# Merging the mixer's work into three bursts per batch instead of four, and moving the low-rank adds to suit

## The chip, the cores and the metric

The kernel runs on one core of a Trainium2 chip. The metric is the device time of one execution in microseconds (us). Kernels are compared only within the same rounds.

Engine names in profile lines: PE is TensorE (matmuls), PEld its weight loads, DVE VectorE, ACT ScalarE, POOL GpSimd, SPq the queue of SyncE, from which all DMA transposes are issued.

## The reference

```python
# 8 batches, S = 3136 rows, D = 256, d_qk = 64, rank 32
scores = (1/S) * z @ z.T
x = u * (relu(scores)**2 @ v)                 # gated attention
h = x.T @ U @ V                               # low rank, along the sequence
w = x + h.T
out = w + relu(w @ w_ch1) @ w_ch2             # channel mixer, 256 -> 1024 -> 256
```

## The kernel before

A batch has 25 tiles of 128 rows (the last has 64). A "turn" computes the attention output of one tile: 24 pairs of matmuls, each 64 rows deep, the two halves of the array running side by side into two PSUM banks (in the trace the two of a pair mostly start 2 to 4 ns apart, and the next pair 109 ns after the first). Two tiles form a pair that shares a set of two banks (`sets[0]`, `sets[1]`, used alternately). (PSUM is the memory that the matmuls here write; its tiles are `ps` in the profile.) The set that no open pair uses is "spare"; low-rank adds and the mixer's down steps use it. The mixer takes a batch in seven chunks of two to four tiles. While the turns of batch b run, the mixer of batch b-1 is put between them, in bursts. After turn 0, the "rank block" (L479) makes `x.T @ U` of batch b-1. `_spread` distributes the score matmuls (`fill`) evenly among the steps of a turn (`main`).

For blocks on one side of the diagonal a turn reads "strips": transposed copies of scores already made, one DMA transpose per turn, issued four turns ahead (five buffers). The same queue also transposes the mixer's input (`turn_x`, tile `ut`, one per chunk) and z of the next batch (`turn_z`, tile `zT`, two pieces).

```python
def turn(b, o):                                  # strip for output tile o
    strip = strip_pool.tile([P, HALF, P], BF16, name="strip")
    transpose(out=strip, in_=A[o][:, P:])        # SP queue, DMA transpose

def close_pair(b, o):
    nc.scalar.copy(out=both[:, :w], in_=banks[1][:, :w])            # L385
    nc.vector.tensor_tensor(both, banks[0], both, add)              # L386
    ...
    nc.vector.tensor_tensor(x_at(b, t0, n), both, u_sb, mult)       # L395

def low_rank(b, c, ps=None, turned=True):        # arguments shortened
    ps = spare() if ps is None else ps
    ...                                          # 4 matmuls into both banks
    for h in range(2):
        nc.vector.tensor_tensor(q, ps[h], q, add)                   # L545
    if turned:
        turn_x(b, c)                             # DMA transpose x -> ut

def extend_z(b):
    zT = zT_of(b)
    nc.vector.tensor_copy(out=zT[:, NT:, :], in_=zT[:, :HALF, :])   # L238
...
burst_at = {4: (0, 1), 8: (2, 3), 13: (4, 5), 17: (6, 7)}
ahead = dict(zip((2, 3, 6, 7, 10, 11, 14), range(NC)))   # turn -> chunk
for i in range(begin, NT):
    o = turns(i)
    ...
        if b and i == 7:
            turn_z(b + 1, ((FIRST, NF),))
        if b and i == 10:
            turn_z(b + 1, ((0, FIRST),))
        if i == 11:
            extend_z(b + 1)
    main = attend_steps(b, o)
    if b and i in ahead:
        main.insert(17 if (i + (i > FIRST)) % 2 == 0 else 10,
                    lambda c=ahead[i]: low_rank(b - 1, c))
    _spread(main, fill)
    ...
        turn(b, turns(i + AHEAD))                # AHEAD = 4
    ...
    for n in burst_at.get(i, ()) if b else ():
        up, down = bursts[n]      # up of chunk n, down of chunk n-1
        steps = [down.pop(0)] if n == 4 else []
        steps += _merge(up, down)
        ...
        run(steps)
```

An up step is four matmuls (line L563) and a ReLU on ACT; a down step is eight matmuls (L608). L371 is attention, L298 scores, L531 low rank, L405 the quarter-size matmuls of the short tile (turn 12).

Of the kernel before, what the change touches and what calls it, by code (L numbers as in the profile page):

```python
# [18 lines left out]
def _spread(main, filler):  # L19

    n, m = len(main), len(filler)
    k = 0
    for i, step in enumerate(main):
        step()
        while k < m and (2 * k + 1) * n <= (i + 1) * 2 * m:
            filler[k]()
            k += 1
    for step in filler[k:]:
        step()


def _merge(*lists):

    keyed = [
        ((i + 0.5) / len(part), n, s)
        for n, part in enumerate(lists)
        for i, s in enumerate(part)
    ]
    return [s for _, _, s in sorted(keyed, key=lambda e: e[:2])]
# [3 lines left out]
def kernel(  # L43
# [28 lines left out]
    FIRST = HALF  # L72
# [27 lines left out]
    def spare():  # L100

        return sets[(opened[0] + (0 if acc else 1)) % 2]
# [29 lines left out]
    def turns(i):  # L132
        return (FIRST + i) % NT
# [4 lines left out]
    def col(t):  # L138
        return place(t) * P
# [10 lines left out]
    NC = len(chunks)  # L150
    offset = {t: (n, k) for n, c in enumerate(chunks) for k, t in enumerate(c)}

    def group(b, c):
        n = len(chunks[c])
        flat = x_bf[:, ((XB // 4) * b + c) % (XR // 4), : n * D]
        return flat.rearrange("p (a t c) -> p a t c", a=ND, c=P)
# [6 lines left out]
    def split(ap):  # L163
        return ap.rearrange("p (t a c) -> p t a c", a=ND, c=P)
# [4 lines left out]
    def load_z(b, parts):  # L169
        if b not in z_raw:  # L170
            z_raw[b] = stage.tile([P, NT, dqk], BF16, name="z_c")
        z_c = z_raw[b]
        for t0, t1 in parts:
            pool_dma(out=z_c[:, t0:t1, :], in_=rows(z[b])[:, t0:t1, :])
            if t1 == NF:
                for r in halves:
                    pool_dma(out=z_c[r, NF, :], in_=z[b, NF * P :, :])
# [14 lines left out]
    def turn_z(b, parts):  # L192
        z_bf = z_tiles[b]
        for t0, t1 in parts:
            transpose(
                out=zT_of(b)[:, t0 : upto(t1), :],
                in_=z_bf[:, t0 : upto(t1), :, :].rearrange("p t h c -> p (t h c)"),
            )
# [37 lines left out]
# [4 lines that stand above are left out]
    def load_v(b, part):  # L240
        t0, t1 = part
        v_bf = v_both[b % 2]
        if t0 < NF:
            pool_dma(out=v_bf[:, t0:t1, :], in_=rows(v[b])[:, t0:t1, :])  # L244
        else:
            for r in halves:
                pool_dma(out=v_bf[r, NF, :], in_=v[b, NF * P :, :])
# [67 lines left out]
    def score_steps(b, j, k0=0, k1=NB):  # L315
        steps = []
        n = (k1 - k0) * P
        parts = _ceil_div(n, 1024)
        each = n // parts
        h = each // 2  # L320
        for i in range(parts):
            at = k0 * P + i * each

            def step(at=at):
                dst = A[j][:, at : at + each].rearrange("p (i h) -> p i h", i=2)
                score(b, [(j, j * P + at + i * h, h, dst) for i in range(2)])

            steps.append(step)
        return steps

    def turn(b, o):
        strip = strip_pool.tile([P, HALF, P], BF16, name="strip")
        transpose(out=strip, in_=A[o][:, P:])
        strips[b, o] = strip
# [165 lines left out]
    def turn_x(b, c):  # L500
        n = len(chunks[c])
        ut = ut_pool.tile([P, ND * 512], BF16, name="ut")
        ut = ut[:, : ND * n * P].rearrange("p (a w) -> p a w", a=ND)
        transpose(
            out=ut.rearrange("p a (t c) -> p (a t) c", c=P),
            in_=group(b, c).rearrange("p a t c -> p a (t c)"),
        )
        uT[c] = ut
# [15 lines left out]
    def low_rank(b, c, ps=None, turned=True):  # L524

        ts = chunks[c]
        ps = spare() if ps is None else ps
        where = [(0, 0), (1, 0)] if len(ts) == 2 else [(0, 0), (0, 1), (1, 0), (1, 1)]
        order = sorted(zip(where, ts), key=lambda e: (e[0][1], e[0][0]))
        for (h, k), t in order:  # L530
            mm(  # L531
                out=ps[h][:, k * D : (k + 1) * D],
                lhsT=V_bf[halves[h], col(t) : col(t) + P],
                rhs=t1[b][halves[h], :],
                start=True,
                stop=True,
            )
        n = len(ts)
        x = group(b, c)
        dst = x.rearrange("p a t c -> p t a c")  # L540
        for h in range(2):
            ks = [k for (g, k), _ in zip(where, ts) if g == h]
            k0 = len(ks) * h if n == 2 else 2 * h
            q = dst[:, k0 : k0 + len(ks)]
            nc.vector.tensor_tensor(out=q, in0=split(ps[h][:, : len(ks) * D]), in1=q, op=ALU.add)  # L545
        if turned:
            turn_x(b, c)
# [92 lines left out]
    def bursts_of(b):  # L640

        out_ = []
        for c in range(NC + 1):
            alone = c == 0 or (c == NC - 1 and b == B - 2)
            up = [lambda s=s, c=c, a=alone: up_steps(c, a)[s]() for s in range(NH // 2)]
            up = up if c < NC else []
            down = down_steps(b, c - 1) if c else []
            out_.append((up, down))
        return out_
# [177 lines left out]
    def run(steps):  # L827
        for s in steps:
            s()
# [5 lines left out]
    for b in range(B):  # L835
        more = b + 1 < B
        begin = 0 if b else 2 * NG
        bursts = bursts_of(b - 1) if b else []
        burst_at = {4: (0, 1), 8: (2, 3), 13: (4, 5), 17: (6, 7)}
        own = own_at if b else first_at  # L840
        v_at = dict(zip((9, 11, 13, 15, 18, 21), V_PARTS[3:]))
        ahead = dict(zip((2, 3, 6, 7, 10, 11, 14), range(NC)))
        for i in range(begin, NT):
            o = turns(i)
            fill = [s for key in own.get(i, ()) for s in score_steps(b, *key)]
            if more:
                fill += [s for key in next_at[i] for s in score_steps(b + 1, *key)]
                if b and i == 1:
                    load_z(b + 1, WHOLE)
# [4 lines that stand above are left out]
                if b == 0 and i in v_at:  # L854
                    load_v(b + 1, v_at[i])
                if i == 11:
                    extend_z(b + 1)
            main = attend_steps(b, o)
            if b and i in ahead:
                main.insert(17 if (i + (i > FIRST)) % 2 == 0 else 10, lambda c=ahead[i]: low_rank(b - 1, c))  # L860
            _spread(main, fill)
            if b == 0 and i in first_turns:
                for t in first_turns[i]:
                    turn(b, t)
            elif i + AHEAD < NT:
                turn(b, turns(i + AHEAD))
            elif more:
                turn(b + 1, turns(i + AHEAD - NT))
            elif i == NT - AHEAD:
                turn_x(b, 0)  # L870
            if b == 0 and i in puts:
                puts[i]()
            if b and i == 0:
                rank_once(b - 1, spare()[0])
            for n in burst_at.get(i, ()) if b else ():
                up, down = bursts[n]
                if not more and n >= NC - 1:
                    late += up + (down if n == NC else [])
                    up, down = [], (down if n < NC else [])

                steps = [down.pop(0)] if n == 4 else []
                steps += _merge(up, down)
                if more:
                    loads = [lambda k=k: load_v(b + 1, V_PARTS[k]) for k in ((n,) if n < NC else (n, n + 1))]
                    steps = _merge(steps, loads)
                    if n == 1:
                        for k, part in ((6, (FIRST, NF)), (3, (0, FIRST))):
                            steps.insert(k, lambda part=part: double_z(b + 1, (part,)))
                run(steps)
# [4 lines left out]
    b = B - 1  # L894
# [45 lines left out]
```

## Time and profile before

| | before |
|---|---|
| median of 3 runs | 1004.49 us |
| PE busy | 984.2 us of 1003.0 (98%) |
| time from one batch's rank block (L479) to the next | 121.24 us, 5 of 6 within 0.25 |
| PE waiting for strips, whole run | 2.7 us |
| granted PE clock | 1.0 |

First, the busy times from the page of the kernel before.

```profile
PE 984.2 (98%) x13688; PEld 776.2 (77%) x13688; DVE 550.6 (55%) x1002; ACT 612.3 (61%) x835; POOL 171.8 (17%) x317
```

The costliest waits of PE in the kernel before: engine, tile and line of the waiting instruction, what it waited for, then us in total, how many times, and the longest.

```profile
PE ps L298 <- ACT A L311: 3.3, 5, 1.0
PE ps L371 <- DMA strip<-A: 2.7, 2, 2.1
PE ps L371 <- DVE A L313: 2.0, 4, 0.9
```

PE is the bottleneck and hardly waits.

Part of the trace that the change aims at: the second of two low-rank adds in successive turns (start in us, duration, engine, line, operation, and how many such instructions were merged into the row). The bracket is PE's idle time and what ended it.

```profile
260.54 0.27 PE L531 MATMUL ps<-t_sb,V_bf 64*128 64x256 bf16 x1
260.96 0.29 PE L531 MATMUL ps<-t_sb,V_bf 64*128 64x256 bf16 x2 [0.16 <-DVE x_bf L545]
```

From start to start PE loses 0.316 us more than usual here; the profile's bracket is smaller because it counts from the modelled end of the matmul before. Below, "gap" means start to start, less the usual distance.

### The profile page before, as it was taken

How to read it: one execution, taken by the hardware profiler on the slowest of the kernel's cores; microseconds unless marked ns; L12 is line 12 of the kernel's file. 1: busy time of each engine (PE TensorE's matmuls, PEld its weight loads, DVE VectorE, ACT ScalarE, POOL GpSimd, SP SyncE). 2: the span in 40 equal slices, each digit the busy share in tenths (PEclk: the TensorE clock that was granted, in tenths of full speed). 3: DMA queues.
4: the chain of work that ended last, by engine and by line, in shares of the span. 5: the costliest groups of instructions: out<-in, count | busy, mean ns of one | idle time of the engine just before them, and what ended most of it. 6: DMA issues, size and time to landing. Idle time of an engine off the chain costs nothing.

```text
span 1003.0 us, 31017 instructions
## 1 busy us (share of the span) xinstructions
PE 984.2 (98%) x13688; PEld 776.2 (77%) x13688; DVE 550.6 (55%) x1002; ACT 612.3 (61%) x835; POOL 171.8 (17%) x317
## 2 busy tenths in 40 slices
PE   7899999999999999999999999999999999999998
PEld 5678777787778877788787887778878788777855
DVE  6868754457544665456644566445663457542342
ACT  7877764667645776466755667466664667633154
POOL 5111112111121211221112211112111120011000
PEclk9999999999999999999999999999999999999999
DMA  9999989999798999999999997989989998678442
GB/s 177 186 196 206 175 153 186 169 198 173 149 205 165 170 160 181 178 179 168 156 185 174 188 162 149 192 177 179 170 156 181 181 183 152 127 152 166 99 98 97
DMA packets 414646, 167.94 MB, mean 167 GB/s; under 512 B 389472, under 2 KB 399136, under 8 KB 414512
## 3 DMA queue, kind: packets, MB, share of 16 engines
q1 hardware_dynamic: 385280, 99.68, 62.9%
q0 software_dynamic: 29232, 66.28, 28.5%
q8 instruction: 107, 1.75, 0.7%
q14 instruction: 27, 0.22, 0.1%
HBM read 61.88 MB, written 25.69 MB: 87 GB/s over the span
## 4 chain that ended last, share of the span: by engine, by line
PE 90%; DVE 4%; ACT 3%; DMA 2%; issue 0%; POOL 0%; DVEq 0%; ACTq 0%; POOLq 0%
PE ps L371 46%; PE ps L608 17%; PE ps L563 17%; PE ps L298 6%; ACT A L311 3%; DVE A L313 1%; PE ps L405 1%; DMA strip<-A 1%; DVE x_bf L545 1%; PE ps L531 1%; DMA z_c<-in_z_dram 1%; PE ps L479 1%; DMA zT<-z_bf 1%; DVE both L386 1%; DVE x_bf L395 0%
## 5 line engine op out<-in xcount | busy, mean ns | idle before, releaser
L311 ACT ACTIVATE A<-ps 128x832 bf16<-128x832 f32 (+9 forms) x477 | 359.1, 768 | 156.1 <-PE ps L298 149.6
L371 PE MATMUL ps<-v,A 64*128 64x256 bf16 x4988 | 341.8, 270 | 2.4 <-DVE A L313 1.1
L313 DVE TENSOR_TENSOR A<-A 128x832 bf16<-128x832 bf16 (+9 forms) x477 | 244.6, 527 | 131.2 <-ACT A L311 128.0
L371 PE MATMUL ps<-v,strip 64*128 64x256 bf16 x4420 | 307.4, 269 | 3.6 <-DMA strip<-A 2.7
L371 PEld LDWEIGHTS <-A 64*128 64x128 bf16 x4988 | 246.8, 94 | 45.8 <-issue 11.2
L581 ACT ACTIVATE relu_bf<-ps 128x1024 bf16<-128x1024 f32 (+2 forms) x206 | 186.0, 911 | 140.8 <-PE ps L563 138.7
L371 PEld LDWEIGHTS <-strip 64*128 64x128 bf16 x4420 | 222.8, 94 | 37.4 <-DMA strip<-A 4.6
L619 DVE TENSOR_TENSOR o_sb<-ps,x_bf 128x512 f32<-128x512 f32 (+1 forms) x104 | 69.7, 670 | 246.2 <-PE ps L608 223.8
L608 PE MATMUL ps<-w_bf,relu_bf 128*128 128x256 bf16 (+1 forms) x1600 | 201.5, 273 | 0.2 <-ACT relu_bf L579 0.2
L563 PE MATMUL ps<-ut,w_bf 128*128 128x512 bf16 (+2 forms) x896 | 198.3, 353 | 1.1 <-DVE x_bf L545 1.0
L608 PEld LDWEIGHTS <-relu_bf 128*128 128x128 bf16 (+1 forms) x1600 | 152.3, 98 | 46.6 <-issue 4.6
L563 PEld LDWEIGHTS <-w_bf 128*128 128x128 bf16 x896 | 85.0, 98 | 63.4 <-issue 7.7
L355 POOL DMA_DIRECT2D u_sb<-in_u_dram x96 | 53.7, 559 | 456.1 <-DVE x_bf L395 440.8
L298 PE MATMUL ps<-zT 64*128 64x416 bf16 (+8 forms) x812 | 131.7, 312 | 0.0
L385 ACT COPY both<-ps 128x512 f32<-128x512 f32 (+1 forms) x104 | 58.9, 566 | 73.8 <-PE ps L371 66.4
L632 POOL DMA_DIRECT2D out_dram<-o_sb x84 | 46.0, 548 | 278.2 <-DVE o_sb L619 274.9
L386 DVE TENSOR_TENSOR both<-ps,both 128x512 f32<-128x512 f32 (+1 forms) x104 | 69.4, 667 | 27.5 <-ACT both L385 26.7
L395 DVE TENSOR_TENSOR x_bf<-both,u_sb 128x512 bf16<-128x512 f32 (+1 forms) x104 | 69.8, 672 | 3.6
L545 DVE TENSOR_TENSOR x_bf<-ps,x_bf 128x512 bf16<-128x512 f32 (+1 forms) x112 | 65.4, 626 | 8.1 <-PE ps L531 8.0
L298 PEld LDWEIGHTS <-zT 64*128 64x128 bf16 x812 | 43.2, 94 | 3.9
L244 POOL DMA_DIRECT2D v<-in_v_dram x61 | 34.1, 561 | 1.2 <-DMA w_bf<-in_moe_w_ch_dram 1.1
L298 PE MATMUL ps<-relu_bf 64*128 64x416 bf16 (+9 forms) x121 | 22.2, 332 | 4.1 <-ACT A L311 3.3
(54 smaller groups left out, 207.9 us busy)
## 6 DMA issues: line engine op xcount, KB each, us to landing
u_sb<-in_u_dram POOLq DMA_DIRECT2D x96, 256.0 KB, 4.1
out_dram<-o_sb POOLq DMA_DIRECT2D x84, 256.0 KB, 3.2
v<-in_v_dram POOLq DMA_DIRECT2D x57, 192.0 KB, 5.1
strip<-A SPq DMA_TRANSPOSE x196, 5.6
out_dram<-o_sb SPq DMA_DIRECT2D x12, 256.0 KB, 2.0
z_c<-in_z_dram POOLq DMA_DIRECT2D x7, 384.0 KB, 5.7
u_sb<-in_u_dram POOLq DMA_DIRECT2D x16, 64.0 KB, 2.9
ut<-x_bf SPq DMA_TRANSPOSE x56, 3.6
```

The costliest lines, as they stand in the source:

```text
L298: mm(out=ps[:, k, :n], lhsT=zT[halves[k], j, :], rhs=zT_flat[halves[k], c : c + n], start=True, stop=True,)
L311: nc.scalar.activation(out=dst, in_=src, func=AF.Relu, scale=sc)
L313: nc.vector.tensor_tensor(out=dst, in0=dst, in1=dst, op=ALU.mult)
L371: mm(out=acc[t0][h][:, (o - t0) * D : (o - t0 + 1) * D], lhsT=w[halves[h]], rhs=v_both[b % 2][halves[h], j, :], start=start, stop=stop, **kw,)
L385: nc.scalar.copy(out=both[:, :w], in_=banks[1][:, :w])
L386: nc.vector.tensor_tensor(out=both[:, :w], in0=banks[0][:, :w], in1=both[:, :w], op=ALU.add)
L395: nc.vector.tensor_tensor(out=x_at(b, t0, n), in0=split(both[:, :w]), in1=u_sb[:, :n, :].rearrange("p t (a c) -> p t a c", c=P), op=ALU.mult,)
L545: nc.vector.tensor_tensor(out=q, in0=split(ps[h][:, : len(ks) * D]), in1=q, op=ALU.add)
L563: mm(out=ps[i][:, :w] if apart else ps[:, i, :w], lhsT=w1_bf[:, db, (hp + i) * P : (hp + i + 1) * P], rhs=uT[c][:, db, len(chunks[c]) * P ...
L581: nc.scalar.activation(out=relus[c][:, hp : hp + 2, :w], in_=ps[:, :, :w], func=AF.Relu)
L608: mm(out=ps[r, k * D : (k + 1) * D], lhsT=relus[c][:, ht, q : q + (TAIL if two else P)], rhs=w2_bf[:, ht, :], start=(ht < 1 + two), stop=( ...
L619: nc.vector.tensor_tensor(out=o_sb[:p, :nk, :].rearrange("p t (a c) -> p t a c", c=P), in0=split(ps[:p, : nk * D]), in1=x_at(b, t, nk)[:p] ...
```

## The change

The intent is fewer changes between attention and mixer on PE, and low-rank adds placed so that every chunk is ready for its earlier burst.

```diff
-        burst_at = {4: (0, 1), 8: (2, 3), 13: (4, 5), 17: (6, 7)}
+        burst_at = {4: (0, 1, 2), 11: (3, 4, 5), 16: (6, 7)}
...
-        ahead = dict(zip((2, 3, 6, 7, 10, 11, 14), range(NC)))
+        ahead = dict(zip((1, 2, 3, 6, 7, 10, 14), range(NC)))
...
-                main.insert(17 if (i + (i > FIRST)) % 2 == 0 else 10, lambda c=ahead[i]: low_rank(b - 1, c))
+                at = 17 if (i + (i > FIRST)) % 2 == 0 or i == 1 else 12
+                main.insert(at, lambda c=ahead[i]: low_rank(b - 1, c))
```

## The prediction

> **What bounds the kernel.** TensorE. The profile's first part has PE busy 984.2 of 1003.0 us (98%), ScalarE 612, VectorE 551; the chain of waits is 90% PE; PE's own waits sum to about 14 us. In the steady state one batch takes 121.3 us (PE's timeline). DMA is busy but PE almost never waits for it.
>
> **What recurs in each of the 7 mixed batches (gaps between matmul starts, PE's timeline).**
> - Attention uses 64-row matmuls, two at a time (about 109 ns a pair); the mixer uses 128 rows (109 ns for 256 columns). Crossing from one form to the other takes 200 to 205 ns instead of 109: about 93 ns lost, near one 94 to 98 ns weight load. [...] The batch has 8 such crossings for four bursts and 2 for the quarter-tile turn (i=12).
> - The second of two consecutive low-rank adds (i=7) stalls 316 ns: its PSUM set waits for VectorE (L545) of i=6.
>
> **The change.** Only order; no instruction is added or removed.
> 1. One burst fewer, and the second burst (after i=11) runs straight into the quarter turn. Crossings fall by three: 3 x 93 ns = 0.28 us a batch, **-2.0 us** in all.
> 2. Low-rank adds of second turns go from step 10 to 12 (some 0.22 us later), and i=6 now has the small chunk: the 316 ns stall should go, **-2.2 us**.
> 3. The first low-rank add is now at i=1, step 17, in the set that i=2 opens. PE reaches that opening about 1.15 us after the add begins (own 0.22, seven pairs, one score). VectorE[...] has a square (L313, 0.59 us) just ahead, then the two adds, 0.69 us each, overlapping slightly: it is done about 1.9 us after the add begins. PE is in order, so it stalls about 0.75 us: **+5.3 us**.
> 4. Bursts after i=11 and i=16 now begin at the end of a pair. Their first down-projection writes bank 1 of the set just closed, which ScalarE must first copy (0.58 us, from 0.1 us after the turn's end); only one up step (0.44 to 0.55 us) covers it: about 0.2 us each, **+2.8 us**.
> The queue of DMA transposes waits for PE far more than the reverse: no cost there.
>
> **Sum.** -4.2 + 8.1: +3.9 us on 1004.49: **1008.4 us**, 8 in 10 between 1002.5 and 1012.5. Chances: faster by over 2% 0.01, within 2% 0.97, slower by over 2% 0.02.
>
> **What would show it.** (1) 21 instead of 28 bursts, with crossings still near 200 ns. (2) No 316 ns gap at low-rank matmuls. (3) PE at L371 waiting for VectorE x_bf (L545), seven times 0.5 to 0.9 us, some 3 us after each rank block: a new line in PE's waits of about 5 us. (4) PE at L608 waiting for ScalarE both (L385), some 13 times about 0.2 us.
>
> **What would make it wrong.** VectorE free earlier at i=1 (the square done before the add) would shrink 3 to 0.2 us and make the change a gain of 1 to 3 us. Stalls on strips, or output stores bunching in a longer burst, would make it worse.

Two passages about the hardware that no trace of this case shows are cut from this text, and the cuts are marked. No term of the sum went with them: -4.2 + 8.1 still comes to +3.9 us. The order that point 3 counts on is seen in the trace of the kernel before: DVE ran two squares (L313, from 258.69 us) and only then the two adds (L545, from 259.63 us), and while the low-rank matmul of 260.96 us waited for DVE, PE started no other: its last start was at 260.54 us.

## More of the kernel before

Now the queue of DMA transposes in the kernel before, from turn 6 to turn 12 of one batch (start in us, duration in the queue, engine, line, operation, and how many such instructions were merged into the row).

```profile
260.94 1.23 SPq L504 DMA_TRANSPOSE ut<-x_bf  x1
262.26 2.47 SPq L333 DMA_TRANSPOSE strip<-A  x1
264.78 1.45 SPq L195 DMA_TRANSPOSE zT<-z_bf  x1
266.33 1.93 SPq L504 DMA_TRANSPOSE ut<-x_bf  x1
268.35 7.08 SPq L333 DMA_TRANSPOSE strip<-A  x3
281.57 1.76 SPq L195 DMA_TRANSPOSE zT<-z_bf  x1
285.33 1.67 SPq L504 DMA_TRANSPOSE ut<-x_bf  x1
```

From 260.9 to 275.4 us the queue is full: two ut, four strips and a zT one behind the other. PE ran the burst after turn 8 from 266.0 to 278.7 us. In those 12.7 us PE needs no strip, so the queue caught up and stood idle from 275.4 to 281.6.

## The result

The changed kernel took 1037.27 us (median of 6 runs, 1035.07 to 1041.62) against 1003.74 us, ratio 1.0335 with a 95% interval of 1.0303 to 1.0368: slower, far above the range. Its batches take 125.0 to 127.5 us (mean 126.4) instead of 121.2. Granted clock: 0.995.

Busy times from the page of the changed kernel:

```profile
PE 992.1 (96%) x13648; PEld 791.3 (76%) x13688; DVE 551.4 (53%) x1002; ACT 612.8 (59%) x835; POOL 171.5 (17%) x317
```

DVE and ACT do the same work. (40 matmul records are missing from this trace, all L563, so PE's real busy time is a little higher.) The waits of PE in the changed kernel:

```profile
PE ps L371 <- DMA strip<-A: 15.0, 10, 3.1
PE ps L608 <- ACT both L385: 4.1, 7, 0.7
PE ps L608 <- DVE both L386: 4.1, 3, 2.3
PE ps L298 <- ACT A L311: 3.2, 5, 1.0
PE ps L371 <- DVE x_bf L545: 2.3, 7, 0.3
```

The rows for L385 and L545 were predicted in kind; their sizes come below. The rows for strips (15.0 us, from 2.7) and for L386 were not. The queue of transposes in the changed kernel, from the last strips before the stretch on, shows why:

```profile
248.15 7.22 SPq L333 DMA_TRANSPOSE strip<-A  x3
274.57 1.21 SPq L504 DMA_TRANSPOSE ut<-x_bf  x1
275.87 1.35 SPq L333 DMA_TRANSPOSE strip<-A  x1
277.28 2.03 SPq L195 DMA_TRANSPOSE zT<-z_bf  x1
279.40 1.75 SPq L504 DMA_TRANSPOSE ut<-x_bf  x1
281.24 7.62 SPq L333 DMA_TRANSPOSE strip<-A  x3
288.95 3.15 SPq L195 DMA_TRANSPOSE zT<-z_bf  x1
292.20 1.26 SPq L504 DMA_TRANSPOSE ut<-x_bf  x1
```

From turn 6 on it is the same order as before, and the durations are alike (strips 7.62 us for three, before 7.08). But PE is no longer in a burst meanwhile: turns 5 to 11 run from 266.7 to 289.3 us without a break, and the next burst comes after turn 11. The queue is filled for 17.1 of the 17.6 us from 274.57 to 292.20 and does not catch up before the second burst.

Before that, it stood idle from 255.4 to 274.57. It works in order (in the rows above from 274.57 us on, each entry starts 0.05 to 0.09 us after the one before it ends), and its next entry was the ut of turn 6's low-rank add, which started as DVE finished that add (at 274.50). So the rest of the long first burst was of no use to it: these 17.1 us had only the 14.7 us from that entry to the end of turn 11, although the whole seven turns last 22.6 us. Two things come late.

First, the strip for turn 11. The last step of an even turn already reads the next turn's strip (it does the short tile for both), so this strip has three turns, not four. In the batch shown, that strip was issued at 281.24 and landed at 286.41, and PE went on at 286.45. The batch before this one shows it worst (timeline of PE, changed kernel):

```profile
161.20 0.28 PE L371 MATMUL ps<-v,strip 64*128 64x256 bf16 x1 [3.05 <-DMA strip<-A]
161.20 2.75 PE L371 MATMUL ps<-v,A 64*128 64x256 bf16 x26
```

Second, the second zT piece. It was issued 6.0 us before turn 11 ended in the kernel before (281.57, end 287.6) and 0.3 us before it here (288.95, end 289.3), and DVE stands at `extend_z` (L238) until it lands (idle for 7.85 us in the batch shown below). The waits of DVE at that line, kernel before and then changed kernel:

```profile
DVE zT L238 <- DMA zT<-z_bf: 3.9, 6, 1.2
```

```profile
DVE zT L238 <- DMA zT<-z_bf: 44.4, 6, 8.1
```

Behind it in DVE's queue is the add that clears the pair closed by turn 11 (L386): it started at 294.60 us, although ACT's copy, its input, was done at 289.98. The second burst's down steps need that bank (changed kernel, 294 to 296 us):

```profile
294.12 0.56 DVE L238 COPY zT<-zT 128x1536 bf16<-128x1536 bf16 x1 [7.85 <-DMA zT<-z_bf]
294.60 0.68 DVE L386 TENSOR_TENSOR both<-ps,both 128x512 f32<-128x512 f32 x1
...
295.33 1.03 PE L608 MATMUL ps<-w_bf,relu_bf 128*128 128x256 bf16 x8 [2.31 <-DVE both L386]
```

There is a third effect. The 26 attention matmuls after the 3.05 us stall show 2.75 us, while the same 26 after a short stall in the next batch show 1.70 us (changed kernel, timeline):

```profile
286.45 0.28 PE L371 MATMUL ps<-v,strip 64*128 64x256 bf16 x1 [0.76 <-DMA strip<-A]
286.46 1.70 PE L371 MATMUL ps<-v,A 64*128 64x256 bf16 x26
```

Two stretches of the changed kernel, one after each of these stalls (busy times by engine; the number after POOL's is the granted PE clock):

```profile
286.40:289.20 2.80, 2.75 (x49) 2.35 (x49) 0.00 (x0) 0.00 (x0) 0.02 (x1) 1.00 1.20 191
161.10:163.60 2.50, 2.40 (x28) 1.83 (x30) 0.00 (x0) 0.00 (x0) 0.00 (x0) 0.61 1.14 221
```

The clock records hold three periods of 3.413 us each at half clock in mid-run, at the strip stalls of 3.2, 3.0 and 2.2 us; the kernel before has none. Each loses half its length at most, 1.7 us (the second began 0.3 us before its stall ended). They start 252.59 us apart, both times 74.0 times their length; why, no run here shows.

Where the time of a batch went, worked out from the starts of the matmuls as actual time less the plain streaming time of each stage (as the matmuls of the kernel before mostly follow each other: 109 ns for 256 columns over 128 rows, for two 64-row matmuls, or for four quarter-size ones; missing records counted in), means of six batches:

| us lost per batch | before | changed |
|---|---|---|
| rank block and turns 1 to 4 | 0.55 | 1.36 |
| turns 5 to 11 without bursts, half clock included | 0.70 (in two parts) | 3.18 |
| turn 12 and the later turns | 0.66 | 0.57 |
| the bursts | 0.15 | 1.92 |
| sum | 2.06 | 7.03 |

The difference of 4.97 times 7 batches is 34.8 us; 33.5 us were measured.

### The profile page after: what moved, and what is told of

Read it like the earlier page. It is cut to its first block, busy times and chain, and to the rows that moved or that the text cites. A ratio compares the mean times of both kernels' runs of the same rounds, so it can differ in the third digit from the quotient of the medians.

```text
span 1034.5 us, 30961 instructions
## 1 busy us (share of the span) xinstructions
PE 992.1 (96%) x13648; PEld 791.3 (76%) x13688; DVE 551.4 (53%) x1002; ACT 612.8 (59%) x835; POOL 171.5 (17%) x317
## 4 chain that ended last, share of the span: by engine, by line
PE 84%; DMA 7%; ACT 4%; DVE 3%; issue 1%; POOL 0%; DVEq 0%; ACTq 0%; POOLq 0%
PE ps L371 43%; PE ps L608 16%; PE ps L563 15%; PE ps L298 6%; DMA strip<-A 5%; ACT A L311 3%; DVE x_bf L545 2%; DMA zT<-z_bf 1%; PE ps L405 1%; DVE A L313 1%; DMA z_c<-in_z_dram 1%; PE ps L531 1%; PE ps L479 1%; ACT both L385 1%; DVE both L386 0%
## 5 line engine op out<-in xcount | busy, mean ns | idle before, releaser
L371 PE MATMUL ps<-v,A 64*128 64x256 bf16 x4988 | 346.3, 271 | 4.5 <-DVE x_bf L545 2.3
L371 PE MATMUL ps<-v,strip 64*128 64x256 bf16 x4420 | 317.1, 270 | 15.8 <-DMA strip<-A 15.0
L313 DVE TENSOR_TENSOR A<-A 128x832 bf16<-128x832 bf16 (+9 forms) x477 | 245.6, 526 | 157.3 <-ACT A L311 154.5
L371 PEld LDWEIGHTS <-A 64*128 64x128 bf16 x4988 | 260.4, 94 | 46.0 <-issue 15.7
L371 PEld LDWEIGHTS <-strip 64*128 64x128 bf16 x4420 | 235.6, 95 | 48.9 <-DMA strip<-A 18.4
L608 PE MATMUL ps<-w_bf,relu_bf 128*128 128x256 bf16 (+1 forms) x1600 | 201.0, 273 | 8.9 <-ACT both L385 4.1
L563 PE MATMUL ps<-ut,w_bf 128*128 128x512 bf16 (+2 forms) x856 | 195.0, 351 | 2.8 <-DVE x_bf L545 1.0
L608 PEld LDWEIGHTS <-relu_bf 128*128 128x128 bf16 (+1 forms) x1600 | 152.4, 98 | 57.5 <-issue 15.8
L298 PE MATMUL ps<-zT 64*128 64x416 bf16 (+8 forms) x812 | 139.4, 312 | 0.0
L563 PEld LDWEIGHTS <-w_bf 128*128 128x128 bf16 x896 | 85.1, 98 | 63.2 <-issue 7.6
L385 ACT COPY both<-ps 128x512 f32<-128x512 f32 (+1 forms) x104 | 58.9, 566 | 93.0 <-PE ps L371 84.4
L386 DVE TENSOR_TENSOR both<-ps,both 128x512 f32<-128x512 f32 (+1 forms) x104 | 69.2, 666 | 35.5 <-ACT both L385 35.1
L545 DVE TENSOR_TENSOR x_bf<-ps,x_bf 128x512 bf16<-128x512 f32 (+1 forms) x112 | 65.4, 626 | 8.5 <-PE ps L531 8.3
L298 PEld LDWEIGHTS <-zT 64*128 64x128 bf16 x812 | 50.7, 94 | 3.3
L238 DVE COPY zT<-zT 128x1536 bf16<-128x1536 bf16 x7 | 3.9, 559 | 44.4 <-DMA zT<-z_bf 44.4
```

Source lines behind the costliest of these rows:

```text
L298: mm(out=ps[:, k, :n], lhsT=zT[halves[k], j, :], rhs=zT_flat[halves[k], c : c + n], start=True, stop=True,)
L313: nc.vector.tensor_tensor(out=dst, in0=dst, in1=dst, op=ALU.mult)
L371: mm(out=acc[t0][h][:, (o - t0) * D : (o - t0 + 1) * D], lhsT=w[halves[h]], rhs=v_both[b % 2][halves[h], j, :], start=start, stop=stop, **kw,)
L386: nc.vector.tensor_tensor(out=both[:, :w], in0=banks[0][:, :w], in1=both[:, :w], op=ALU.add)
L545: nc.vector.tensor_tensor(out=q, in0=split(ps[h][:, : len(ks) * D]), in1=q, op=ALU.add)
L563: mm(out=ps[i][:, :w] if apart else ps[:, i, :w], lhsT=w1_bf[:, db, (hp + i) * P : (hp + i + 1) * P], rhs=uT[c][:, db, len(chunks[c]) * P ...
```

## The experiments

Theory S: the time is lost because the stretch between the first and the second burst became seven turns long, and the transpose queue, which is full in that stretch (from turn 6 into the second burst: five strips, three ut, two zT), has no burst in which to catch up. Rivals: L, the moved low-rank adds cost it (through DVE and the in-order queue); D, a three-chunk burst floods the DMA and so delays strips; V, DVE held up at `extend_z` is the root of it all.

### e1: the low-rank moves alone

```diff
-        burst_at = {4: (0, 1, 2), 11: (3, 4, 5), 16: (6, 7)}
+        burst_at = {4: (0, 1), 8: (2, 3), 13: (4, 5), 17: (6, 7)}
```

(The diffs of e1 to e4 are against the changed kernel.)

> The four bursts of the kernel before (after turns 4, 8, 13, 17), with the changed places of the low-rank adds. Theory S (the DMA transposes are starved of time between the burst after turn 4 and the one after turn 11): the loss goes but for the new stall of 0.70 us at the opening of turn 2, less the 0.32 us stall that is gone, times 7: 1005 to 1010 us, granted clock 1.0, PE waits for strips under 4 us. Rival L (the moved low-rank adds cost the time, through VectorE and the in-order DMA queue): stays above 1025 us.

Measured: 1007.75 us, ratio 1.0021 (0.999 to 1.0052), as S expected; clock 1.0, strip waits 3.7 us. A batch takes 121.95 us, 0.71 more than before. L falls. What the low-rank moves cost is the predicted wait at the opening of turn 2 (gap 0.70 us in every batch); their gain is small: the 0.316 us gap at turn 7 is gone but a gap of 0.165 us came at the opening of turn 8.

### e2: the first burst merged, but a burst after turn 8 kept

```diff
-        burst_at = {4: (0, 1, 2), 11: (3, 4, 5), 16: (6, 7)}
+        burst_at = {4: (0, 1, 2), 8: (3,), 13: (4, 5), 17: (6, 7)}
```

> First burst of three chunks (0-2) as in the change, but chunk 3 alone keeps its burst after turn 8, then 4-5 after 13 and 6 after 17. S: even one chunk (about 5 us) between turns 8 and 9 lets the transposes catch up: strip waits under 5 us in all, 1004 to 1011 us. Rival D (a three-chunk burst floods the DMA with V loads and output stores, which delays the strips whatever comes later): strip waits of 10 us or more stay, over 1018 us.

Measured: 1031.23 us, ratio 1.0237 (1.018 to 1.0294): the time I expected is missed by 20 us, and whether the loss reaches 2% is unclear from the runs. Yet the strip waits did fall to 3.2 us, as S said and D did not. The lost time came through the other late transpose, as PE's waits in this run show:

```profile
PE ps L371 <- DVE both L386: 16.9, 6, 3.2
...
PE ps L371 <- DMA strip<-A: 3.2, 4, 1.1
```

The timeline of the same run at one of these stalls:

```profile
295.56 0.56 DVE L238 COPY zT<-zT 128x1536 bf16<-128x1536 bf16 x1 [5.00 <-DMA zT<-z_bf]
296.04 0.68 DVE L386 TENSOR_TENSOR both<-ps,both 128x512 f32<-128x512 f32 x1
...
296.77 0.94 PE L371 MATMUL ps<-v,A 64*128 64x256 bf16 x14 [2.55 <-DVE both L386]
```

The one-chunk burst lasts 5.8 us, against 12.7 us before. That was enough for the strips, not for the zT behind them (issued at 289.23). Here no burst follows turn 11, so turn 13 at once needs the bank that DVE has not cleared. All six stalls are 2.7 to 3.3 us and a half-clock period starts within 0.9 us of the end of each (granted clock of the profiled run: 0.989). So S as I had written it was too narrow: it is not only strips that come late, and the worst consequence depends on what stands behind the late transpose.

### e3: zT transposed during the second burst

```diff
-                if b and i == 7:
-                    turn_z(b + 1, ((FIRST, NF),))
-                if b and i == 10:
-                    turn_z(b + 1, ((0, FIRST),))
...
-                if i == 11:
+                if i == 12:
                     extend_z(b + 1)
...
+                if more and n == 3:
+                    turn_z(b + 1, ((FIRST, NF),))
+                    turn_z(b + 1, ((0, FIRST),))
                 up, down = bursts[n]
```

> The changed kernel with its three bursts, but the two zT transposes for the next batch are issued at the start of the second burst (not in turns 7 and 10), and the copy that extends zT goes to turn 12. S: five strips, three ut and two zT took some 21 us of queue time in five turns of 15.5 us; without the zT it is about 16: strip waits under 4 us, no half-clock windows, and the burst's wait for VectorE (L386) gone: 1009 to 1016 us (the 0.70 us at turn 2 and the 0.72 us at the third burst stay, 7 times each). Rivals L and D: stays above 1025 us.

Measured: median 1017.08 us, ratio 1.0137 (1.0076 to 1.0199), one of four runs at 1028.31. The median is just over the expected range; the profiled run (1015.65 us) has these top waits of PE:

```profile
PE ps L608 <- ACT both L385: 4.1, 7, 0.7
PE ps L371 <- DMA strip<-A: 3.7, 3, 2.4
```

The waits for L386 are gone, strips are back to the level of e1, and there is no half clock in the steady state. With three bursts and three chunks in two of them kept, L and D cannot explain that. Two of six batches still lose 0.8 and 0.9 us to a strip in turn 10; no run shows why only these two.

### e4: only `extend_z` later

```diff
-                if i == 11:
+                if i == 12:
                     extend_z(b + 1)
```

> The changed kernel with only the VectorE copy that extends zT moved from turn 11 to turn 12, so that VectorE does not sit behind a late zT transpose when it must clear the pair closed by turn 11. S: the burst's waits for VectorE (L386, 0.8 us a batch on average) go, strip waits of about 1.8 us a batch and half-clock windows stay: 1026 to 1033 us. If the blocked VectorE was the root of everything (rival V): under 1016 us.

Measured: 1031.37 us, ratio 1.0255 (1.0218 to 1.0293), as S expected. PE's waits for L386 are gone, strip waits stay:

```profile
PE ps L371 <- DMA strip<-A: 13.9, 7, 2.8
```

The clock is 0.991 in the profiled run, with four half-clock periods in mid-run. V falls as the root in the changed kernel: the blocked DVE is one of two consequences of the late queue. Removing it alone recovers about 6 us of the 33 by the medians, about 8 by the ratios. Together with e3, which shares this edit and its runs of the kernel before, it shows that moving the two zT transposes out of the crowded stretch is what counts, about 14 us more by the medians, 12 by the ratios.

### e5: as e3, with the third burst back after turn 17

```diff
-        burst_at = {4: (0, 1, 2), 11: (3, 4, 5), 16: (6, 7)}
+        burst_at = {4: (0, 1, 2), 11: (3, 4, 5), 17: (6, 7)}
```

> The run with the zT transposes in the second burst, with one more edit: the third burst goes back from turn 16 to turn 17, where a pair is half done and its other set has long been copied. If the 0.73 us gap at the start of that burst is ScalarE's copy of the closed pair (queued behind a score activation of 0.86 us), it goes: 5 us less than the run before it, 1.008 to 1.010 of the kernel before.

Measured: 1013.43 us, ratio 1.0038 (1.0 to 1.0076), better than expected. (The profiled run, 1009.84 us, is the fastest of the six.) The gap at the third burst is gone in every batch; the stage lost 0.83 us in e3 and loses 0.11 here. In the changed kernel, the gap looked like this:

```profile
451.35 0.86 ACT L311 ACTIVATE A<-ps 128x832 bf16<-128x832 f32 x1 [0.18 <-PE ps L298]
...
452.11 0.58 ACT L385 COPY both<-ps 128x512 f32<-128x512 f32 x1
...
452.74 1.03 PE L608 MATMUL ps<-w_bf,relu_bf 128*128 128x256 bf16 x8 [0.56 <-ACT both L385]
```

The copy starts only when the score activation ahead of it is done.

### e6: as e5, with the first three low-rank adds in turns 2, 3, 4

```diff
-        ahead = dict(zip((1, 2, 3, 6, 7, 10, 14), range(NC)))
+        ahead = dict(zip((2, 3, 4, 6, 7, 10, 14), range(NC)))
```

> As e5, and the first three low-rank adds go from turns 1, 2, 3 to turns 2, 3, 4, so that no add precedes the opening of turn 2 in the same set. The 0.70 us gap there goes, and about 0.15 us of the 0.23 us at turn 4; the add in turn 4 may cost up to 0.5 us at the burst that follows it. Net 2 to 5 us less than e5: 1.003 to 1.007 of before.

Measured: 1006.79 us, ratio 0.998 (0.9943 to 1.0017), better than expected. The stage of turns 1 to 4 loses 0.55 us again, as in the kernel before. For comparison, the opening of turn 2 in the changed kernel, which this edit removes:

```profile
236.81 0.59 DVE L313 TENSOR_TENSOR A<-A 128x832 bf16<-128x832 bf16 x1 [0.68 <-ACT A L311]
...
237.43 1.29 DVE L545 TENSOR_TENSOR x_bf<-ps,x_bf 128x512 bf16<-128x512 f32 x2
...
238.78 0.70 PE L371 MATMUL ps<-v,A 64*128 64x256 bf16 x9 [0.33 <-DVE x_bf L545]
```

### e7: the kernel before, with one number changed

```diff
-                main.insert(17 if (i + (i > FIRST)) % 2 == 0 else 10, lambda c=ahead[i]: low_rank(b - 1, c))
+                main.insert(17 if (i + (i > FIRST)) % 2 == 0 else 12, lambda c=ahead[i]: low_rank(b - 1, c))
```

> The kernel before with one number changed: low-rank adds of second turns at step 12 instead of 10. The low-rank-only run showed that the 0.316 us gap inside the add at turn 7 turns into 0.165 us at the opening of turn 8. Net 0.1 to 0.2 us a batch, about 1 us: 0.997 to 1.000 of before, which the timing may not resolve; the trace's batch period should fall from 121.24 to about 121.1 us.

Measured: 1003.64 us, ratio 0.9961 (0.9911 to 1.0012). The period is 121.02 us in four of six batches, against 121.24: a gain of 0.22 us a batch, 1.5 us in all, seen in the trace but not resolved by the timing. The other two batches take 121.74 and 121.92 us.

### e8: as e6, with two up steps at the head of the second burst

```diff
                 steps = [down.pop(0)] if n == 4 else []
+                if n == 3:
+                    steps = [up.pop(0), up.pop(0)]
```

> As e6, and the second burst begins with two up steps instead of one, so that ScalarE's copy of the pair closed by turn 11 is done when the first down step needs its bank. The gap of 0.19 us there goes: about 1.3 us less than e6. If the strips keep up, three crossings fewer (0.28 us a batch) then make it equal to before or faster: 0.997 to 1.004; a batch period of about 121.2 us.

Measured: 1003.94 us, ratio 0.9962 (0.9922 to 1.0001). The second burst loses 0.19 us less than in e6. Two of six batches take 121.02 and 121.11 us; the others have extra gaps of 0.2 to 0.6 us, mostly in turns 5 to 11. So three bursts can be as fast as four, and perhaps a little faster; e7 reaches the same with one number. Neither is shown to beat the kernel before beyond the noise.

## Why the prediction was wrong

- **Crossings** (-2.0 us): right in kind. Crossings that remain still take about 0.20 us, and 21 bursts remain. The e8 batch of 121.02 us is consistent with the gain, but no run isolates it, and e7 reaches 121.02 us with four bursts.
- **The 316 ns stall** (-2.2 us): mis-sized in sum. The stall went, but 0.165 us of it came back at the opening of turn 8, and the gap at the opening of turn 4 grew from 0.10 to 0.23 us. The single-number run e7 gained 0.22 us a batch, 1.5 us.
- **The add at turn 1** (+5.3 us): right. The gap at the opening of turn 2 is 0.70 us (0.75 predicted) in all 7 batches; e1 isolates it and e6 removes it.
- **Bursts at the end of a pair** (+2.8 us): half right. After turn 11 the gap is 0.19 us as predicted; after turn 16 it is 0.73 us in six of the seven batches, because ACT's copy stands behind a score activation of 0.86 us. I had taken the start of the copy from a turn without scores. This adds 0.5 us a batch.
- **"The queue of DMA transposes waits for PE far more than the reverse: no cost there."** This step failed, and it alone is most of the miss. It is true of the whole run and false of the stretch that the change lengthens. In the kernel before, the queue was full for 14.5 us from turn 6 on, and the burst after turn 8 was the time in which it caught up. The change takes that burst away. Late strips cost gaps of 0.6 to 3.2 us at the end of turn 10 (together 12.3 us over the seven batches), late zT held DVE and through it the second burst (4.6 us in three batches), and the clock was halved at three stalls (about 5 us): together some 22 of the 28.9 us by which the prediction was too low. e3 shows it: the same bursts, with the two zT transposes moved into one of them and `extend_z` a turn later, got rid of about 20 us. The prediction did name strip stalls as a thing that would make it worse, but gave them no size.

What stays open is why the queue is slow in that stretch: whether the transposes' own rate or other DMA traffic sets it. No run separates the two. More traffic than before is not the reason: all DMAs of the core together moved 196 GB/s while the queue was full in the kernel before (260.94 to 275.43 us) and 174 GB/s in the changed one (274.57 to 292.20), of which the transposes' own packets made 142 and 139; three strips took 7.08 and 7.62 us. Also open is what an earlier start of the queue would give, with turn 6's low-rank add elsewhere. Part of the strips' remaining unsteadiness in e5, e6 and e8 (0 to 1.8 us in a batch) is not explained either.

## What to carry to other kernels

A burst of work that does not need a queue's results is that queue's time to catch up; before merging or moving it, add up the queue's work in the stretch that remains and compare it with the time from when its first entry can start (here 14.7 of 22.6 us), not with the whole run. Averages of "who waits for whom" hide this. When a late transfer also stands at the head of an in-order engine's queue, look at what waits behind it, and allow for a half-clock period with each stall of 2 to 3 us on PE (12 of the 15 stalls over 2 us in the mixed batches of the changed kernel, e2 and e4 brought one; granted clocks of the profiled runs 0.995, 0.989 and 0.991).

## Three measurements on the hardware

- Gaps and half clock. In the changed kernel a gap of 2.2 us was followed by a half-clock period of 3.413 us, while a gap of 2.5 us in another batch was not. What separates them comes out when the mixed batches of its trace (100 to 960 us) are cut into stretches of 3.413 us in step with its half-clock periods, and PE's gaps over 0.15 us are summed in each stretch. The three stretches that a half-clock period followed had 2.95, 2.64 and 2.20 us of gaps; every other one had at most 1.95 us. The gap of 2.5 us lay across two stretches. Three periods of one trace do not make a rule.
- Weight loads and crossings. In full-row runs of the kernel before the load is hidden (L608: 109 ns from start to start with loads of 98 ns). At the crossings between 64-row and 128-row matmuls 198 to 206 ns pass instead, about 203 on average. What the extra 94 ns are, no run here shows.
- DMA transposes. One strip, 128 x 1536 elements of 2 bytes or 393 KB, took 1.3 to 5.5 us in the queue (median 2.1, kernel before), and 2.5 us on average in the crowded stretch shown above (7.62 us for three, changed kernel), which makes about 155 GB/s, an estimate from time in the queue.
